# Attention in quarter tiles of the array, and mixing in plain float32

## The chip, the cores and the metric

The kernel runs on one core of a Trainium2 chip. TensorE multiplies matrices (weights are loaded first, then the moving operand streams through), ScalarE computes activations, VectorE elementwise operations, GpSimd (POOL) and SyncE (SP) mostly issue DMAs. The metric is device time in microseconds, the median of several runs.

## The reference, cut to what matters

```python
# attention: q, k, v are (4, 12, 448, 64)
scores = scale * np.matmul(q, k.transpose(0, 1, 3, 2))
scores = cap * np.tanh(scores / cap)
scores = scores - np.max(scores, axis=-1, keepdims=True)
attn = np.exp(scores)
attn = attn / (np.sum(attn, axis=-1, keepdims=True) + 1e-09)
x = np.matmul(attn, v)                  # then to (4, 448, 768)
# mixing over the tokens, rank 32, then two big products
xt = x.transpose(0, 2, 1)
h = xt @ U @ V                          # U (448, 32), V (32, 448)
u = x + h.transpose(0, 2, 1)
ch = np.maximum(u @ w_ch1, 0.0) @ w_ch2 # (768, 3072), (3072, 768)
out = u + ch
```

## The kernel before, in words

The program first lists tasks (`Plan.task`), each with engines, assumed durations, a priority and a mode (the tile shape on TensorE; a change of mode is charged `SWITCH`). `simulate` walks through time, always starting on a free engine the ready task of the lowest priority number for which buffers are free. The order that comes out is the order of instructions on each engine, so each engine's queue runs in that fixed order. `RANK` shifts priorities by kind of task, `SLOW` stretches some assumed DMA latencies.

There are 24 head pairs (4 batches, 6 pairs of 2 heads, 64 wide each). `four` handles four pairs at a time, `normalize` and `mixin` two pairs at a time; two pairs are called a half here, and there are twelve.

Scores (L488 to 495): keys lie on the output partitions. Of the 448 keys of a pair three tiles have 128 keys, and the two heads use the upper and the lower 64 rows of the array (two 64x128 matmuls side by side). The last 64 keys of two pairs share a narrow tile of four 64x64 matmuls (`t == 3`). So a half has seven tiles, two of which fill one buffer `th` of 128 x 1792. ScalarE applies tanh to each tile (L498) and exp to the buffer (L508).

P.V (L518 to 537): `rest` does the last 64 keys of two pairs in four 64x64 matmuls into two accumulators `o`, `o2`, then `full` does, for each pair, three tiles of 128 keys in two 128x64 matmuls each (two heads side by side in the array's columns). VectorE adds the exps up into `es` for the row sums (L540). Each accumulator is copied to `u` by ScalarE or VectorE (L555). From `SUMS` on the narrow tile is not added on VectorE, but summed on TensorE (L576).

Row sums (L571 to 577) are matmuls with ones, 128x32. Their reciprocals go through three small DMAs on POOL (`spread`, `put`, `get`) and scale `u` (`norm`, L602).

Mixing (`mixin`, L607 to 667): two transposes of `u` (112 tokens at a time, four matmuls each), a copy as fp32r `high`, the remainder `low` on VectorE (L635), `products` with U in four fp32r matmuls for each of the two steps (L640), the copy `ys` and its remainder (L651), `mix` with V, 128x128, in fp32r (L660), and the sum into `u` (L664).

The big products (L851, L916, L1049), seven products in place of eight, need PSUM banks of the score tiles and so begin when the attention is done with them; the last mixings run among them. Their operands are made on ScalarE and VectorE by `operands`, `strassen_weights` and `weights`, partly under the attention. The last block's outputs are added to `u` by VectorE, or copied by ScalarE and added by an accumulating DMA of POOL (`onto`, L1076).

## Time and profile before

| | us |
|---|---|
| median of 3 runs | 858.47 (857.27 to 858.69) |
| the profiled execution | 853.6 |
| its span, first to last instruction | 851.8 |
| TensorE busy | 840.4 (99%) |
| VectorE busy | 691.0 (81%) |
| ScalarE busy | 527.6 (62%) |
| POOL busy | 146.1 (17%) |

The shares are means over stages. A stretch of the windows view gives the busy time of each engine in one stage. On the timeline of TensorE the end of a matmul is modelled, so the step from a start to the next start says more than a duration; a count in a chunk is instructions, and a float32 matmul is two of them. In a row, `128*64` is rows by columns of the array that a matmul uses.

### The profile page before, as it was taken

To read this page: it belongs to the slowest core of one execution; us is meant where nothing else is said; L and a number is where in the kernel's file an instruction comes from. 1 tells how busy PE (TensorE), PEld (TensorE's weight loads), DVE (VectorE), ACT (ScalarE), POOL (GpSimd) and SP (SyncE) were. 2 spreads that over 40 slices of the span, in tenths; PEclk is the share of its full clock that TensorE was granted. 3 is DMA by queue.
4 is the path that set the end of the run, shared out by engine and by line. 5 is a ranking of instruction groups with operands and counts; after the bars stand their busy time and mean duration, and the time that the engine had idled before them with its cause. 6 is when DMAs were issued, how large, how long until landed. Compare 5 with 4: busy or idle time off the path is not lost. (4 is left out here: it accounts for less than half of the span.)

```text
span 851.8 us, 11737 instructions
## 1 busy us (share of the span) xinstructions
PE 840.4 (99%) x4264; PEld 671.4 (79%) x4264; DVE 691.0 (81%) x1144; ACT 527.6 (62%) x789; POOL 146.1 (17%) x188
## 2 busy tenths in 40 slices
PE   9999999998999999999999999999999999999998
PEld 5334334346899999999999899999999999999997
DVE  2799889999887777877778699789888788888786
ACT  7999899885555355545555465456655555656472
POOL 0111111111022122122122122102111111111142
PEclk9999999999999999999999999999999999999999
DMA  6752443423578878787877866714427354262479
GB/s 225 241 172 84 160 148 96 146 68 93 183 190 259 245 188 249 191 265 211 231 231 207 252 162 151 215 48 120 114 36 179 68 143 93 53 170 42 122 136 224
DMA packets 51354, 136.51 MB, mean 160 GB/s; under 512 B 6720, under 2 KB 27104, under 8 KB 51296
## 3 DMA queue, kind: packets, MB, share of 16 engines
q1 hardware_dynamic: 23024, 79.29, 28.3%
q0 software_dynamic: 21360, 37.59, 24.6%
q10 hardware_dynamic: 6912, 18.88, 5.7%
q8 instruction: 33, 0.54, 0.3%
q14 instruction: 25, 0.20, 0.1%
HBM read 79.28 MB, written 24.47 MB: 122 GB/s over the span
## 5 line engine op out<-in xcount | busy, mean ns | idle before, releaser
L851 PE MATMUL mm<-x,ws 128*128 128x448 f32 x1512 | 332.7, 367 | 1.4 <-ACT cx L284 0.8
L851 PEld LDWEIGHTS mm<-x,ws 128*128 128x128 f32 x1512 | 283.3, 188 | 27.3 <-ACT cx L284 1.2
L916 PE MATMUL mm<-g,w 128*128 128x448 f32 x864 | 187.0, 366 | 0.6 <-DVE cx L864 0.3
L916 PEld LDWEIGHTS mm<-g,w 128*128 128x128 f32 x864 | 162.0, 188 | 15.0 <-ACT st L284 0.9
L1049 PE MATMUL mm<-g,w 128*128 128x448 f32 x696 | 154.9, 366 | 0.0
L284 ACT ACTIVATE st<-mm 128x448 f32<-128x448 f32 x133 | 72.4, 544 | 113.7 <-PE mm L916 55.2
L1049 PEld LDWEIGHTS mm<-g,w 128*128 128x128 f32 x696 | 130.6, 188 | 11.8
L929 POOL DMA_DIRECT2D u<-st x72 | 62.5, 868 | 268.9 <-ACT st L284 263.8
L1084 POOL DMA_DIRECT2D u<-st x57 | 49.4, 866 | 224.1 <-ACT st L284 161.4
L498 ACT ACTIVATE th<-sc,qsc 128x896 f32<-128x896 f32 x84 | 80.3, 1005 | 11.9 <-PE sc L493 11.7
L493 PE MATMUL sc<-qk 64*128 64x448 f32 (+1 forms) x384 | 77.8, 573 | 0.0
L508 ACT ACTIVATE th<-th,capt 128x1792 f32<-128x1792 f32 x42 | 75.2, 1790 | 0.8
L921 DVE TENSOR_TENSOR u<-u,mm 128x448 f32<-128x448 f32 x72 | 44.5, 618 | 21.6 <-PE mm L916 19.9
L534 PE MATMUL o<-th,vn 128*64 128x448 f32 x288 | 59.4, 548 | 0.0
L493 PEld LDWEIGHTS sc<-qk 64*128 64x128 f32 (+1 forms) x384 | 27.2, 175 | 37.2 <-issue 18.9
L343 DVE SCALAR_TENSOR_TENSOR wa<-wa,wr 128x768 int32<-128x768 int32 (+2 forms) x50 | 46.7, 935 | 11.1 <-ACT wa L335 10.3
L698 DVE TENSOR_TENSOR ws<-ta,ws 128x384 fp32r<-128x384 f32 x96 | 53.0, 552 | 3.2 <-ACT ws L284 2.9
L1079 DVE TENSOR_TENSOR u<-u,mm 128x448 f32<-128x448 f32 x57 | 35.0, 619 | 23.3 <-PE mm L1049 21.7
L540 DVE TENSOR_TENSOR es<-es,th 128x896 f32<-128x896 f32 (+1 forms) x44 | 47.5, 1082 | 6.0 <-ACT th L508 5.5
L335 ACT ACTIVATE wa<-wr 128x768 f32<-128x768 f32 (+2 forms) x50 | 44.1, 884 | 3.8 <-DVE wr L340 2.4
L534 PEld LDWEIGHTS o<-th,vn 128*64 128x64 f32 x288 | 18.5, 136 | 32.8 <-issue 30.0
L284 ACT ACTIVATE ws<-ta 128x384 fp32r<-128x384 f32 x64 | 32.9, 519 | 15.2 <-PE mm L851 8.9
(118 smaller groups left out, 957.5 us busy)
## 6 DMA issues: line engine op xcount, KB each, us to landing
wr<-in_w SPq DMA_DIRECT2D x48, 768.0 KB, 5.7
u<-st POOLq DMA_DIRECT2D x129, 224.0 KB, 4.1
kept<-wa ACTq DMA_DIRECT2D x48, 384.0 KB, 5.8
qk<-in_qk SPq DMA_DIRECT2D x24, 448.0 KB, 4.0
wr<-kept SPq DMA_DIRECT2D x24, 384.0 KB, 3.7
wa<-kept SPq DMA_DIRECT2D x24, 384.0 KB, 4.0
vn<-in_v SPq DMA_DIRECT2D x12, 448.0 KB, 3.7
rb<-rd POOLq DMA_DIRECT2D x24, 224.0 KB, 3.7
```

The lines of the kernel that those rows point to most:

```text
L284: e.activation(out=out, in_=in_, func=func)
L493: nc.tensor.matmul(ps.t[out, a, :S], qks[c].t[hd, 1, 128 * t:min(S, 128 * t + 128)], qks[c].t[hd, 0], start=True, stop=True)
L498: nc.scalar.activation(out=th.t[:, j], in_=ps.t[:, :, :S], func=AF.Tanh, scale=self.qsc)
L508: nc.scalar.activation(out=th.t, in_=th.t, func=AF.Exp, scale=self.capt)
L534: nc.tensor.matmul(o.t[64 * a:64 * a + 64, :S], vn.t[:, 3 * i + t, a], th.t[:, j, a], start=False, stop=t == 2)
L540: e.tensor_tensor(out=out(), in0=in0(), in1=in1(), op=ALU.add)
L698: e.tensor_tensor(out=lo, in0=src(), in1=hi.bitcast(F32), op=ALU.subtract)
L851: nc.tensor.matmul(ps.t[:, :S], ws[p].t[:, wi, sl], xs[p].t[:, xi, d], start=fresh and n == 0, stop=n == 8, skip_group_check=not fresh)
L916: nc.tensor.matmul(ps.t[:, :S], w1[f].t[:, wi, sl], g[b, f].t[:, gi], start=f == fs[0] and i == 0, stop=f == fs[-1] and i == 2)
L929: nc.gpsimd.dma_start(out=u.t[:, d], in_=st.t, accum_op=ALU.add)
L1049: nc.tensor.matmul(ps.t[:, :S], w[:, wi, k, sl], g[gi][:, k], start=fresh and n == 0, stop=n == 5, skip_group_check=not fresh)
L1084: self.task({"POOL": 1000}, lambda: nc.gpsimd.dma_start(out=out(), in_=st.t, accum_op=ALU.add), r=[(st, 0)], w=[key], lat=6000, prio=-200)
```

## The change

Score tiles have 64 keys of each of the two pairs of a half: all seven are four 64x64 matmuls, a quarter of the array each. P.V runs tile by tile in the same shape, as seven tasks that all write both accumulators; V is laid out accordingly by the host. The exps of both pairs are summed in one `es`, all seven tiles on VectorE (`SUMS` is now past the last pair). The row sums are two 128x64 matmuls. The mixing is in plain float32: no remainders, all four token blocks in one `xx`, then eight products of 112x64, and a mix of four 64x64 matmuls for both pairs of a half; `ys` no longer shares the buffer of `sr`. The planner's priorities are set by stage and by half, U and V are kept as plain float32, the order of the first operands changes, and three more outputs of the last block are added by VectorE.

```diff
...
-EARLY = 5, 6, 2, 3, 4, 1, 7
+EARLY = 5, 6, 2, 3, 1, 7, 4
 
 ALONE = 12
-SUMS = 20
+SUMS = 24
...
-        self.an = Pool("an", {"sr": 1, "rb": 1}, side="right", shared={"ys": "sr"})
+        self.an = Pool("an", {"sr": 1, "rb": 1, "ys": 1}, side="right")
...
-        ust = self.ust = self.buf("ust", [TM, KT, 4, R], F32R, self.aq)
-        vst = self.vst = self.buf("vst", [128, S], F32R, self.aq)
+        ust = self.ust = self.buf("ust", [TM, KT, 4, R], F32, self.aq)
+        vst = self.vst = self.buf("vst", [128, S], F32, self.aq)
...
-            for i in range(3):
-                nc.vector.tensor_copy(ust.t[:, :, i], ur)
-            nc.vector.tensor_tensor(out=ust.t[:, :, 3], in0=ur, in1=ust.t[:, :, 0].bitcast(F32), op=ALU.subtract)
+            nc.vector.memset(ust.t[:, :, 1], 0.0)
+            nc.vector.tensor_copy(ust.t[:, :, 0], ur)
 
         def v_parts():
-            vr = a2.t[:, :S]
-            nc.vector.tensor_copy(vst.t, vr)
-            nc.vector.tensor_tensor(
-                out=vst.t[64:96], in0=vr[64:96], in1=vst.t[64:96].bitcast(F32), op=ALU.subtract)
+            nc.vector.tensor_copy(vst.t, a2.t[:, :S])
...
-        steps = [(0, 0), (0, 1), (0, 2), (1, 3), (1, 0), (1, 1), (1, 2), (2, 0), (2, 1), (3, 3), (2, 2), (3, 0), (3, 1), (3, 2)]
         where = {}
         for g in range(7):
             th = self.buf("th", [128, 2, 2, S], F32, *pools)
             pss = [self.psum("sc", 2), self.psum("sc2", 2)]
-            prio = prios[steps[2 * g][0]]
+            prio = prios[4 * g // 14 * 2]
             for j in range(2):
-                i, t = steps[2 * g + j]
-                where[i, t] = th, j
+                h, t = divmod(2 * g + j, 7)
+                where[h, t] = th, j
                 ps = pss[j]
-                cs = (i - 1, i) if t == 3 else (i,)
-
-                def scores(i=i, t=t, ps=ps, cs=cs):
-                    for c in cs:
-                        out = slice(64 * (c % 2), 64 * (c % 2) + 64) if t == 3 else slice(0, 128)
+
+                def scores(h=h, t=t, ps=ps):
+                    for i in range(2):
+                        qk = qks[2 * h + i]
                         for a in range(2):
                             hd = slice(64 * a, 64 * a + 64)
                             nc.tensor.matmul(
-                                ps.t[out, a, :S], qks[c].t[hd, 1, 128 * t:min(S, 128 * t + 128)], qks[c].t[hd, 0],
-                                start=True, stop=True)
+                                ps.t[64 * i:64 * i + 64, a, :S], qk.t[hd, 1, 64 * t:64 * t + 64], qk.t[hd, 0], start=True, stop=True)
...
-                r = [(qks[c], 0) for c in cs]
+                r = [(qks[2 * h + i], 0) for i in range(2)]
                 if j == 0:
-                    self.task({"PE": 750}, scores, r=r, w=[(ps, 0), (pss[1], "next")], prio=prio, mode="q" if t == 3 else "sc")
+                    self.task({"PE": 750}, scores, r=r, w=[(ps, 0), (pss[1], "next")], prio=prio, mode="q")
                 else:
-                    self.task({"PE": 750}, scores, r=[*r, (pss[1], "next")], w=[(ps, 0)], prio=-300, mode="q" if t == 3 else "sc")
+                    self.task({"PE": 750}, scores, r=[*r, (pss[1], "next")], w=[(ps, 0)], prio=-300, mode="q")
...
         for h in range(2):
-            vn, prio, i0 = vns[h], prios[2 * h], 2 * h
-            rth, rj = self.rest[p + i0 + 1] = where[i0 + 1, 3]
+            vn, prio, q = vns[h], prios[2 * h], p + 2 * h
+            whole = q + 1 < SUMS
+            ths = [where[h, t] for t in range(7)]
             os = [self.psum("o"), self.psum("o2")]
-
-            def rest(vn=vn, os=os, rth=rth, rj=rj):
-                for i in range(2):
-                    rows = slice(64 * i, 64 * i + 64)
-                    for a in range(2):
-                        nc.tensor.matmul(
-                            os[i].t[64 * a:64 * a + 64, :S], vn.t[rows, 6, a], rth.t[rows, rj, a], start=True, stop=False)
-
-            self.task({"PE": 760}, rest, r=[(vn, 0), (rth, rj)], w=[(o, 0) for o in os], prio=prio, mode="q")
-            for i, o in enumerate(os):
-                es = self.es[p + i0 + i] = self.buf("es", [128, 2, S], F32, *pools)
-                ts = [where[i0 + i, t] for t in range(3)]
-
-                def full(i=i, o=o, vn=vn, ts=ts):
-                    for t in range(3):
-                        th, j = ts[t]
+            es = self.es[q + 1] = self.buf("es", [128, 2, S], F32, *pools)
+            if not whole:
+                self.rest[q + 1] = ths[6]
+            at = lambda k: (lambda th=k[0], j=k[1]: th.t[:, j])
+            total = lambda es=es: es.t
+            for t in range(7):
+
+                def full(t=t, os=os, vn=vn, ths=ths):
+                    th, j = ths[t]
+                    for i in range(2):
+                        rows = slice(64 * i, 64 * i + 64)
                         for a in range(2):
                             nc.tensor.matmul(
-                                o.t[64 * a:64 * a + 64, :S], vn.t[:, 3 * i + t, a], th.t[:, j, a], start=False, stop=t == 2)
-
-                self.task({"PE": 2250}, full, r=[(vn, 0), *ts], w=[(o, 0)], prio=prio, mode="av")
+                                os[i].t[64 * a:64 * a + 64, :S], vn.t[rows, t, a], th.t[rows, j, a], start=t == 0, stop=t == 6)
+
+                self.task({"PE": 750}, full, r=[(vn, 0), ths[t]], w=[(o, 0) for o in os], prio=prio, mode="q")
 
                 def add(e, in0, in1, out):
                     e.tensor_tensor(out=out(), in0=in0(), in1=in1(), op=ALU.add)
 
-                at = lambda k: (lambda th=k[0], j=k[1]: th.t[:, j])
-                whole = lambda es=es: es.t
-                self.task({"DVE": 1090}, partial(add, in0=at(ts[0]), in1=at(ts[1]), out=whole), r=ts[:2], w=[(es, 0)],
-                    prio=prio, lock=True)
-                self.task({"DVE": 1090}, partial(add, in0=whole, in1=at(ts[2]), out=whole), r=ts[2:], w=[(es, 0)],
-                    prio=prio, lock=True)
-                if p < SUMS:
-                    rows = slice(64 * i, 64 * i + 64)
-                    some = lambda es=es, rows=rows: es.t[rows]
-                    self.task({"DVE": 1090}, partial(add, in0=some, in1=lambda rows=rows, rth=rth, rj=rj: rth.t[rows, rj], out=some),
-                        r=[(rth, rj)], w=[(es, 0)], prio=prio, lock=True)
-                b, q = divmod(p + i0 + i, NP)
-                u = self.u_bufs[b]
-                self.task({"DVE": 620, "ACT": 560}, lambda e, q=q, o=o, u=u: self.copy(e, u.t[:, q], o.t[:, :S]), r=[(o, 0)],
-                    w=[(u, q)], prio=prio)
+                if t and (whole or t < 6):
+                    self.task({"DVE": 1090}, partial(add, in0=at(ths[0]) if t == 1 else total, in1=at(ths[t]), out=total),
+                        r=ths[:2] if t == 1 else [ths[t]], w=[(es, 0)], prio=prio, lock=True)
+            b, q = divmod(q, NP)
+            u = self.u_bufs[b]
+            for i, o in enumerate(os):
+                self.task({"DVE": 620, "ACT": 560}, lambda e, q=q + i, o=o, u=u: self.copy(e, u.t[:, q], o.t[:, :S]), r=[(o, 0)],
+                    w=[(u, q + i)], prio=prio)
...
-        e = self.es[p - 1], self.es[p]
-        rth, rj = self.rest[p]
+        e = self.es[p]
         rest = p >= SUMS
+        rth, rj = self.rest.get(p, (e, 0))
...
         def sums():
-            for i in range(4):
-                nc.tensor.matmul(
-                    s.t[32 * i:32 * i + 32, :S], self.ones[:, 0], e[i % 2].t[:, i // 2], start=True, stop=not rest)
-            for i in range(4 if rest else 0):
-                nc.tensor.matmul(
-                    s.t[32 * i:32 * i + 32, :S], self.ones[:, 1 + i % 2], rth.t[:, rj, i // 2], start=False, stop=True)
+            half = self.ones[:, 1:].rearrange("p i r -> p (i r)")
+            for a in range(2):
+                nc.tensor.matmul(s.t[64 * a:64 * a + 64, :S], half, e.t[:, a], start=True, stop=not rest)
+            for a in range(2 if rest else 0):
+                nc.tensor.matmul(s.t[64 * a:64 * a + 64, :S], half, rth.t[:, rj, a], start=False, stop=True)
...
         u = self.u_bufs[b]
-        yp = None
         ks = [(u, 2 * pp), (u, 2 * pp + 1)]
+        xx = self.buf("xx", [TM, KT, 256], F32, self.aq)
         for t0 in (0, 2):
             tp = self.psum("misc")
-            yp = yp or self.psum("misc")
-            xx = self.buf("xx", [TM, 2, 2, 256], F32R, self.aq)
...
-            def view(tp):
-                return tp.t[:TM].rearrange("p (t n) -> p t n", t=2)
-
-            def high(e, tp=tp, xx=xx):
-                self.copy(e, xx.t[:, 0], view(tp))
-
-            def low(tp=tp, xx=xx):
-                nc.vector.tensor_tensor(out=xx.t[:, 1], in0=view(tp), in1=xx.t[:, 0].bitcast(F32), op=ALU.subtract)
-
-            def products(t0=t0, xx=xx):
+            def high(e, t0=t0, tp=tp):
+                self.copy(e, xx.t[:, t0:t0 + 2], tp.t[:TM].rearrange("p (t n) -> p t n", t=2))
+
+            self.task({"PE": 450}, transposes, r=[*ks, ("ident", 0)], w=[(tp, 0)], prio=prio, mode="mm")
+            self.task({"ACT": 600, "DVE": 690}, high, r=[(tp, 0)], w=[(xx, t0)], prio=prio)
+        yp = self.psum("misc")
+
+        def products():
+            for j in range(KT):
+                w = self.ust.t[:, j, :2].rearrange("p i r -> p (i r)")
                 for i in range(2):
-                    for j in range(2):
-                        nc.tensor.matmul(
-                            yp.t[:, :256], self.ust.t[:, t0 + j], xx.t[:, i, j], start=t0 + j + i == 0,
-                            stop=t0 + j == KT - 1 and i == 1)
-
-            self.task({"PE": 450}, transposes, r=[*ks, ("ident", 0)], w=[(tp, 0)], prio=prio, mode="mm")
-            self.task({"ACT": 600, "DVE": 690}, high, r=[(tp, 0)], w=[(xx, 0)], prio=prio)
-            self.task({"DVE": 690}, low, r=[(tp, 0), (xx, 0)], w=[(xx, 1)], prio=prio)
-            self.task({"PE": 480}, products, r=[(xx, 0), (xx, 1), (self.ust, 0)], w=[(yp, 0)], prio=prio, mode="mm")
-        ys = self.buf("ys", [128, 256], F32R, self.an)
-
-        def y_low():
-            nc.vector.tensor_tensor(
-                out=ys.t[32:64], in0=yp.t[32:64, :256], in1=ys.t[32:64].bitcast(F32), op=ALU.subtract)
-
-        self.task({"ACT": 380, "DVE": 400}, lambda e: self.copy(e, ys.t, yp.t[:, :256]), r=[(yp, 0)], w=[(ys, 0)], prio=prio)
-        self.task({"DVE": 420}, y_low, r=[(yp, 0)], w=[(ys, 0)], prio=prio)
+                    nc.tensor.matmul(
+                        yp.t[64 * i:64 * i + 64, :128], w, xx.t[:, j, 128 * i:128 * i + 128], start=j == 0, stop=j == KT - 1)
+
+        ys = self.buf("ys", [128, 128], F32, self.an)
+        self.task({"PE": 860}, products, r=[(xx, 0), (xx, 2), (self.ust, 0)], w=[(yp, 0)], prio=prio, mode="av")
+        self.task({"ACT": 270, "DVE": 220}, lambda e: self.copy(e, ys.t, yp.t[:, :128]), r=[(yp, 0)], w=[(ys, 0)], prio=prio)
+        hh = [self.psum("misc") for _ in range(2)]
+
+        def mix():
+            for i in range(2):
+                rows = slice(64 * i, 64 * i + 64)
+                for c in range(2):
+                    cs = slice(64 * c, 64 * c + 64)
+                    nc.tensor.matmul(hh[i].t[cs, :S], ys.t[rows, cs], self.vst.t[rows], start=True, stop=True)
+
+        self.task({"PE": 750}, mix, r=[(ys, 0), (self.vst, 0)], w=[(hh[0], 0), (hh[1], 0)], prio=prio, mode="q")
         for i in range(2):
-            hh = self.psum("misc")
-
-            def mix(i=i, hh=hh):
-                nc.tensor.matmul(hh.t[:, :S], ys.t[:, 128 * i:128 * i + 128], self.vst.t, start=True, stop=True)
-
-            def add(i=i, hh=hh):
+
+            def add(i=i):
                 x = u.t[:, 2 * pp + i]
-                nc.vector.tensor_tensor(out=x, in0=x, in1=hh.t[:, :S], op=ALU.add)
-
-            self.task({"PE": 210}, mix, r=[(ys, 0), (self.vst, 0)], w=[(hh, 0)], prio=prio, mode="mm")
-            self.task({"DVE": 620}, add, r=[(hh, 0)], w=[ks[i]], prio=prio)
+                nc.vector.tensor_tensor(out=x, in0=x, in1=hh[i].t[:, :S], op=ALU.add)
+
+            self.task({"DVE": 620}, add, r=[(hh[i], 0)], w=[ks[i]], prio=prio)
...
-                self.onto(ps, out, key, n % 2 if not final else n < 15)
+                self.onto(ps, out, key, n % 2 if not final else n < 12)
...
-            if -150 < t.prio < 0:
-                t.prio += next((r for x, r in RANK if stage.startswith(x)), 0)
+            if -150 < t.prio < -70:
+                p = t.prio + 100
+                x, early, late = next((r for r in RANK if stage.startswith(r[0])), ("", 0, 0))
+                t.prio += (early if p < ALONE else late) + SHIFT.get(x, {}).get(p, 0)
...
```

## Rows read from the trace of the kernel before

**Rows 1.** Windows: stretch, length, PE, PEld, DVE, ACT, POOL busy us (instructions), clock, DMA share, GB/s

```profile
43.00:197.00 154.00, 152.38 (x874) 61.65 (x875) 140.63 (x206) 139.82 (x140) 22.83 (x39) 1.00 0.41 124
60.00:180.00 120.00, 119.03 (x680) 48.11 (x680) 109.96 (x159) 111.78 (x114) 17.73 (x31) 1.00 0.38 115
197.00:225.00 28.00, 25.25 (x141) 21.17 (x140) 26.57 (x50) 16.90 (x33) 2.34 (x4) 1.00 0.28 88
225.00:500.00 275.00, 274.44 (x1349) 252.64 (x1348) 214.13 (x373) 140.19 (x242) 52.15 (x60) 1.00 0.81 230
```

**Rows 2.** Timeline of TensorE, one half of the steady stage: start us, us, line, shape, count

```profile
74.44 0.96 PE L573 MATMUL misc<-es,ones 128*32 128x448 f32 x8
75.33 0.65 PE L624 MATMUL misc<-ident,u 128*112 128x128 f32 x4
75.91 0.98 PE L522 MATMUL o<-th,vn 64*64 64x448 f32 x8
76.82 1.77 PE L493 MATMUL sc<-qk 64*128 64x448 f32 x8
78.52 0.74 PE L640 MATMUL misc<-xx,ust 112*128 112x256 f32 x4
79.10 0.60 PE L624 MATMUL misc<-ident,u 128*112 128x128 f32 x4
79.63 2.48 PE L534 MATMUL o<-th,vn 128*64 128x448 f32 x12
82.04 0.74 PE L640 MATMUL misc<-xx,ust 112*128 112x256 f32 x4
82.71 1.94 PE L493 MATMUL sc<-qk 64*128 64x448 f32 x12
84.58 2.48 PE L534 MATMUL o<-th,vn 128*64 128x448 f32 x12
86.98 0.68 PE L660 MATMUL misc<-vst,ys 128*128 128x448 f32 x2
87.59 1.77 PE L493 MATMUL sc<-qk 64*128 64x448 f32 x8
89.30 0.96 PE L573 MATMUL misc<-es,ones 128*32 128x448 f32 x8
```

**Rows 3.** Timeline of TensorE: sums of another half and of the eighth after it

```profile
58.49 0.96 PE L573 MATMUL misc<-es,ones 128*32 128x448 f32 x8
...
182.84 0.96 PE L573 MATMUL misc<-es,ones 128*32 128x448 f32 x8
183.61 0.94 PE L576 MATMUL misc<-th,ones 128*32 128x448 f32 x8
184.48 1.77 PE L493 MATMUL sc<-qk 64*128 64x448 f32 x8
```

**Rows 4.** Timeline of TensorE's weight loads in one 128x64 chunk, third wave on

```profile
45.53 0.14 PEld L534 LDWEIGHTS o<-th,vn 128*64 128x64 f32 x2 [0.23 <-issue]
45.91 0.14 PEld L534 LDWEIGHTS o<-th,vn 128*64 128x64 f32 x2 [0.23 <-issue]
```

**Rows 5.** Groups by line and form: busy us, mean ns of one, idle before

```profile
L498 ACT ACTIVATE th<-sc,qsc 128x896 f32<-128x896 f32 x84 | 80.3, 1005 | 11.9 <-PE sc L493 11.7
L508 ACT ACTIVATE th<-th,capt 128x1792 f32<-128x1792 f32 x42 | 75.2, 1790 | 0.8
L540 DVE TENSOR_TENSOR es<-es,th 128x896 f32<-128x896 f32 x24 | 26.1, 1086 | 5.6 <-ACT th L508 5.5
L635 DVE TENSOR_TENSOR xx<-misc,xx 112x512 fp32r<-112x512 f32 x24 | 16.4, 681 | 1.1 <-ACT xx L284 0.8
L651 DVE TENSOR_TENSOR ys<-misc,ys 32x256 fp32r<-32x256 f32 x12 | 5.0, 418 | 0.4
L286 DVE COPY u<-o 128x448 f32<-128x448 f32 x15 | 9.3, 622 | 3.7 <-PE o L534 3.6
```

**Rows 6.** Timeline of TensorE behind the attention: start us, us, idle before

```profile
204.55 0.51 PE L640 MATMUL misc<-xx,ust 112*128 112x256 f32 x2 [0.70 <-ACT xx L284]
```

120 lines of the change are left out of this document (77 added, 43 removed).

## Prediction

> **What bounds the kernel now.** I read the windows by stage first, to see which engine has no time left in each. From 43 to 197 us, the steady stage of the attention, TensorE is busy 152.38 of 154.00 us, VectorE 140.63 and ScalarE 139.82 [rows 1]. From 225 us on the products of the last block hold it, 274.44 of the next 275 us [rows 1]; the change touches none of these products, so what it can move lies ahead of 225 us. The granted clock is 1.00 (the level of 2.4 GHz) in every stretch of the table, so no term here is a term of the clock.
>
> A busy TensorE need not work at its peak, so the second view is its timeline in the steady stage, of which I use only the step from one start to the next start. One half of a group of four head pairs (four heads, two pairs) repeats between two row sums. Its steps [rows 2]: sums 0.89, transposes 0.58 and 0.53, rest of P.V 0.91, the two full P.V chunks 2.41 and 2.40, mixing products 0.58 and 0.67, a chunk of two score tiles 1.70, a chunk of one full and one narrow score tile 1.87, mix 0.61. Seven score buffers fill in two halves, two of them mixed, so a mean half has 2.5 x 1.70 + 1.87 = 6.12 of scores. The sum is 0.89 + 1.11 + 0.91 + 4.81 + 1.25 + 6.12 + 0.61 = 15.70 us. Eight halves in a row took (182.84 - 58.49) / 8 = 15.54 us each [rows 3]. So the period is the sum of TensorE's steps to 1%: nobody else sets it.
>
> What is in a step? A P.V chunk of three tiles takes 2.41, the rest chunk of one tile 0.91 [rows 2]: a tile costs (2.41 - 0.91) / 2 = 0.75, and a chunk 0.16 more, once. That 0.16 is what a change of tile shape costs: the mixed score chunk, with a change inside, is 0.17 longer than the plain one, 1.87 against 1.70 [rows 2]. A mean half has 3.5 score chunks, one change inside, and nine other chunks, so 13.5 changes or about 2.2 us, a seventh of the period.
>
> **The change, part by part.** *Tiles.* Scores and P.V keep their number of tiles, seven and seven a half, each now four 64x64 matmuls where a full one was two. The rest chunk is such a tile, 0.91 alone, and so 0.75 and one 0.16 if it splits as the full ones do. The trace never shows two quarter tiles back to back; bounds 0.75 and 0.91 each. I take 0.75, from the row nearest to it: within a 128x64 chunk the loads of the next wave issue 0.38 us apart, 45.53 and 45.91, the stream time of a wave, and hide [rows 4]. The Trainium skill speaks against this: "TensorE: Matmul & The Clock Gate", Part 3 (row and column tiling), says that a weight load overlaps running matmuls only when its row group differs, and quarter tiles share row groups in twos. The 128x64 chunk above shares them too, and its rows do not agree; by the rule the result would be rival B.
>
> *Changes of shape.* Scores, P.V and the mix now have one shape, so a half leaves it only for sums, transposes and products: three excursions, in and out, 6 x 0.16 = 0.96; with the two transposes apart 8 x 0.16 = 1.28.
>
> *Sums.* Two 128x64 matmuls for four 128x32, the price of one tile: 0.75 (the old chunk 0.89 less 0.16 is 0.73) [rows 2].
>
> *Mixing.* Transposes as before, 1.11 less two changes, 0.79. The products become eight float32 matmuls of 128 columns, two at a time: by the stream, 4 x 0.75 x 128/448 = 0.86. If their sixteen loads do not hide, the nearest row is the transposes chunk, four loads in 0.53 - 0.16 = 0.37, so 1.48. I take 1.0, nearer to the stream, since loads hid in the 128x64 chunk. The mix is one more quarter tile, 0.75 for 0.61.
>
> *A half after:* 15 x 0.75 + 0.75 + 0.79 + 1.0 = 13.79, and 0.96 to 1.28 of changes: 14.75 to 15.07, against 15.70. I take 14.85, so -0.85. The window of 154 us holds ten mixings and ten halves of P.V: -8.5 us (bounds, with those of the products and the changes: 15.55 and 14.61 a half, -1.5 to -11).
>
> *The other engines under it.* VectorE loses both subtractions of the mixing, 2 x 0.681 and 0.418 a half [rows 5], 1.8 us, or 18 us of its 140.63. ScalarE has (80.3 + 75.2) / 12 = 12.96 us of tanh and exp a half that nothing removes [rows 5]. From 60 to 180 us it was busy 111.78 of 120.00 [rows 1], 14.48 in 15.54, so 1.5 us a half were copies and the like; at 14.85 all of it still fits, at 97%, and copies can go to VectorE, which has just been given 1.8. The cover is gone near a period of 13.5 to 14.5, not at 14.85.
>
> *Last row sums.* The last two halves summed their rest on TensorE, 0.87 each (183.61 to 184.48) [rows 3]; that goes, -1.7 us, and four VectorE adds of 1.086 more take its place [rows 5]. They lie beside the last P.V, under the 18 us that VectorE was given; uncovered they cost up to 4.3.
>
> *Start.* The first score tile needs two head pairs instead of one. The program issues the second load right behind the first. No row shows the gap between their landings; between 0 and a score chunk, 1.70 [rows 2], I take +0.5, nearer to 0, since the program loads the scale of the first tanh between the two.
>
> *Behind the attention.* Two mixings run among the big products, whose shape the old mixing shared (128 wide). The new ones leave it: products 1.0 + 0.32 against 1.25 less two changes, 0.93, mix 0.75 + 0.32 against 0.61 less one, 0.45: +0.39 and +0.62, so +1.0 each, +2.0. Against that stand waits for the two-step copies, 0.70 at 204.55 and one more like it [rows 6], in a stretch with 25.25 of 28.00 us busy [rows 1]: -1.0, bounds 0 and -2.7.
>
> *The rest.* The order in which operands of the big products are made, their priorities, and three sums of the last block that move from ScalarE and POOL's accumulating DMA to VectorE: TensorE is full beside them (274.44 of 275), so 0 within 1 either way. No DMA is added; POOL's and SP's queues keep their entries. Rank, shift and latency tables only reorder.
>
> *New waits.* Both P.V accumulators now end on the same tile, and the next half's first P.V tile waits for both copies, 0.622 each [rows 5]; the mix needs two misc banks at once, and the products wait for both transposed copies. Behind such a wait all of TensorE's queue stands, and ScalarE's tanh behind that. Old steps show three chunks between a half's last P.V and the next rest chunk (86.98, 87.59, 89.30) [rows 2], which cover it. Bounds 0 and 1 us a half, taken as +1.0 in all.
>
> *Sum:* -8.5 - 1.7 + 0.5 + 2.0 - 1.0 + 1.0 = -7.7, about -8 us. The profiled execution took 853.6 us (span 851.8 and 1.8 around it), so 846 by its measure. The median of the runs is 858.47, 4.9 above it; the same -8 there gives 850.5.
>
> **The rivals.** *A: ScalarE takes over as the bound.* If its share of copies stays, 14.48 a half, and it gets no further than 96% busy, a half takes 15.1: gain (15.54 - 15.1) x 10 = 4.5, 854. For it: the lowest idle after TensorE's in the stretch from 60 to 180 us [rows 1]. Against: every copy has a VectorE form, and score tiles of 0.75 reach it sooner than behind chunks of 2.41.
>
> *B, slower: quarter tiles do not stream.* Each pays its own 0.16, as the lone rest chunk did: 15 x 0.91 + 0.75 + 0.79 + 1.0 and 3 x 0.16 for the excursions is 16.67, +0.97 on 15.70, ten halves, +9.7; with the other terms (+0.8) 869. It decides from the point where a tile costs 0.82 and not 0.75: 15 x 0.07 eats the 1.0 that the shapes give. For it: eight loads and eight matmuls in 0.75 us, twice as dense as before. The Trainium skill's rule on loads, named above, points the same way. Against: the loads at 45.53 and 45.91 [rows 4].
>
> *C: the new waits eat it.* One copy and its two latencies uncovered a half, 0.8 to 1 us: 858.5, no change. For it: in-order queues, and the same two banks for every mixing step. Against: only 1.6 of 154 us idle before, with as many hand-overs.
>
> **How the numbers follow.** Forecast 0.62, 850.5 (845 to 855 by the bounds that are likely together); A 0.14; B 0.08; C 0.13; anything else slower 0.03. A measurement of this kernel can tell about 0.2%, 1.7 us, from no change. Faster: forecast and A, 0.76. Same: most of C, 0.12. Slower: B, the rest, a little of C, 0.12. The range takes in the forecast's bounds, A, and C's middle, 843.5 to 859.0, and leaves out B and the far end of C.
>
> **What would show it.** Right: two adjacent quarter tiles on TensorE step 0.75 apart and 1.5 for two; from one half's row sums to the next 14.7 to 15.1; six to eight changes of shape a half; the first big product at about 188 us, and not at 197, where the steady window ends [rows 1]; products step near 1.2 with the change; VectorE less busy over the attention. Wrong: quarter tiles at 0.9; TensorE idle ahead of P.V or the mix with a copy as releaser; ScalarE at 97% or more; the attention shorter, but the big products later idle for weights or operands.

## The result, and the profile after

| | before | after |
|---|---|---|
| median of five runs, us | 857.47 (854.75 to 858.69) | 864.92 (862.11 to 869.60) |
| profiled execution, us | 853.6 | 862.11 |
| its span, us | 851.8 | 860.3 |
| first big product of the last block, us | 196.69 | 205.75 |

The ratio is 1.0099, with a 95% interval of 1.0075 to 1.0123: the kernel became slower by 1%, where 850.5 was forecast and the range ended at 859.0.

The first view is the page of the changed kernel, engine by engine: busy us, share of the span, instructions.

```profile
PE 838.8 (97%) x4944; PEld 671.0 (78%) x4944; DVE 679.1 (79%) x1122; ACT 522.5 (61%) x776; POOL 143.7 (17%) x185
```

TensorE was busy 838.8 us, and 840.4 before, while the span grew by 8.5. VectorE, at 679.1, has time to spare. So time was lost that is not work. The windows of the changed kernel say where (stretch, length, busy us of PE, PEld, DVE, ACT, POOL with instructions, granted clock, DMA share, GB/s); the first and third answer to [rows 1].

```profile
43.00:197.00 154.00, 142.72 (x1356) 58.27 (x1352) 126.24 (x181) 131.40 (x129) 21.16 (x37) 0.99 0.41 125
139.00:147.00 8.00, 7.18 (x60) 3.90 (x64) 7.75 (x13) 4.33 (x5) 1.35 (x3) 0.79 0.04 5
197.00:225.00 28.00, 27.29 (x196) 19.35 (x189) 24.43 (x44) 21.62 (x37) 3.92 (x7) 1.00 0.33 105
240.00:260.00 20.00, 16.82 (x74) 14.89 (x74) 14.56 (x27) 10.21 (x19) 4.32 (x5) 0.91 0.73 189
```

In the steady stage TensorE is idle for 11.28 of 154 us; before it was 1.62 [rows 1]. No other engine took its place as the bound: VectorE and ScalarE are less busy than before too. What grew is waiting. The attention as a whole is 9.06 us longer (205.75 against 196.69 at the first big product), and from there to the end the two kernels take the same time, 654.6 and 655.1 us of their spans. The loss is all in the attention. The rows of TensorE that set its end, first of the kernel before, then of the changed one:

```profile
104.16 0.96 PE L573 MATMUL misc<-es,ones 128*32 128x448 f32 x8
...
196.69 2.09 PE L851 MATMUL mm<-x,ws 128*128 128x448 f32 x9
198.71 0.96 PE L573 MATMUL misc<-es,ones 128*32 128x448 f32 x8
...
204.84 0.97 PE L588 MATMUL misc<-es,ones 128*64 128x448 f32 x4 [0.45 <-DVE es L561]
205.75 2.09 PE L858 MATMUL mm<-x,ws 128*128 128x448 f32 x9
```

Now the timeline of TensorE in a half of the changed kernel that goes well, the answer to [rows 2] (start us, us, line, shape, count):

```profile
71.34 0.97 PE L588 MATMUL misc<-es,ones 128*64 128x448 f32 x4
72.24 0.98 PE L555 MATMUL o<-th,vn 64*64 64x448 f32 x8
...
77.53 1.75 PE L519 MATMUL sc<-qk 64*64 64x448 f32 x16
79.21 1.09 PE L650 MATMUL misc<-xx,ust 112*64 112x128 f32 x16
80.24 0.98 PE L555 MATMUL o<-th,vn 64*64 64x448 f32 x8
81.04 0.93 PE L663 MATMUL misc<-vst,ys 64*64 64x448 f32 x8
81.79 1.68 PE L519 MATMUL sc<-qk 64*64 64x448 f32 x16
83.29 2.44 PE L555 MATMUL o<-th,vn 64*64 64x448 f32 x24
85.66 0.60 PE L588 MATMUL misc<-es,ones 128*64 128x448 f32 x2
```

By the step from one start to the next: the sums 0.90, three P.V tiles 2.37, two score tiles 1.50 (81.79 to 83.29), the mix 0.75, the products 1.03. A tile of four small matmuls costs 0.75 wherever the next step has its shape. The half takes 14.32 us; eight halves of before took 15.54 each [rows 3]. The row sums of all twelve halves stand at 25.65, 39.39, 55.92, 71.34, 85.66, 99.07, 119.96, 134.06, 158.16, 172.25, 191.73 and 204.84. Before, the sixth stood at 104.16 and the twelfth at 198.71. So the changed kernel was 5.1 us ahead after six halves, and lost 11.2 over the next six (105.8 against 94.6). The remaining 2.9 are nine big products that before ran ahead of its last sums, and none does now. Three of the late halves are long: 20.9, 24.1 and 19.5 us.

What stands in them? The same view from the last score tile ahead of the first long gap to the sums at its end (a bracket is idle time before the step, and what ended it), with SyncE's queue below it:

```profile
107.89 0.93 PE L519 MATMUL sc<-qk 64*64 64x448 f32 x8
108.65 0.92 PE L555 MATMUL o<-th,vn 64*64 64x448 f32 x4
110.41 4.35 PE L555 MATMUL o<-th,vn 64*64 64x448 f32 x42 [0.85 <-ACT u L316]
114.24 0.58 PE L519 MATMUL sc<-qk 64*64 64x448 f32 x2
114.60 0.54 PE L555 MATMUL o<-th,vn 64*64 64x448 f32 x2
114.61 2.03 PE L519 MATMUL sc<-qk 64*64 64x448 f32 x14
117.02 0.98 PE L519 MATMUL sc<-qk 64*64 64x448 f32 x8 [0.37 <-ACT th L523]
118.84 0.98 PE L555 MATMUL o<-th,vn 64*64 64x448 f32 x8 [0.84 <-ACT th L533]
119.96 0.97 PE L588 MATMUL misc<-es,ones 128*64 128x448 f32 x4
...
108.85 1.21 SPq L495 DMA_DIRECT2D qk<-in_qk  x2
```

The score tile at 107.89 is the last that reads the two q/k buffers of its half; at 108.85 SyncE issues the loads into them, the first of which is for the second pair of the next half. The next score tile, which needs that pair, runs at 114.24. Until then TensorE has only P.V tiles left, six in a row (48 instructions, one of them behind a wait of 0.85 for the copy of an accumulator). Then score tile, tanh and exp run one behind the other, with TensorE waiting for the tanh at 117.02 and for the exp at 118.84: the last P.V tile of the half lies in the same exp as the first of the next. From 107.89 to 119.96 the steps hold 88 instructions, 44 small matmuls of one shape or eleven tiles, with one change at the end 8.4 us; they took 12.1: 3.7 lost. The same place in the next long half shows the wait for the load itself:

```profile
151.14 0.93 PE L519 MATMUL sc<-qk 64*64 64x448 f32 x4
152.45 1.72 PE L519 MATMUL sc<-qk 64*64 64x448 f32 x12 [0.38 <-DMA qk<-in_qk]
155.21 0.98 PE L519 MATMUL sc<-qk 64*64 64x448 f32 x8 [1.04 <-ACT th L523]
157.03 0.98 PE L555 MATMUL o<-th,vn 64*64 64x448 f32 x8 [0.84 <-ACT th L533]
158.16 0.97 PE L588 MATMUL misc<-es,ones 128*64 128x448 f32 x4
```

Four tiles and a change of shape, 3.2 us by the steps, in 7.0 (151.14 to 158.16): 3.8 lost. The third long half has the same four tiles in 6.7 us, from 185.05 to 191.73, with 0.73 of wait for the load: 3.5 lost. The three together lose 11.0 us.

The second place stands in the same trace: TensorE, VectorE and POOL around 139 us.

```profile
134.96 1.73 PE L519 MATMUL sc<-qk 64*64 64x448 f32 x16
139.82 1.96 PE L635 MATMUL misc<-ident,u 128*112 128x128 f32 x8 [3.13 <-DVE u L615]
141.71 1.67 PE L555 MATMUL o<-th,vn 64*64 64x448 f32 x8
143.20 1.67 PE L519 MATMUL sc<-qk 64*64 64x448 f32 x16
144.81 1.09 PE L650 MATMUL misc<-xx,ust 112*64 112x128 f32 x16
...
138.67 1.09 DVE L615 TENSOR_TENSOR u<-u,rb 128x896 f32<-128x896 f32 x1 [3.73 <-DMA rb<-rd]
...
130.72 1.05 POOL L610 DMA_DIRECT2D rb<-rd  x2 [3.98 <-DMA rd<-r]
```

The transposes of the mixing need the attention scaled by the row sums, and the sums go to DRAM and come back spread over the partitions, by POOL's DMA. The DMA, whose issue took from 130.72 to 131.77, let the scaling start at 138.67, about 7 us later where 3.7 is the median. TensorE's queue has the transposes next, and stands for 3.13 us. What follows is slow as well: transposes 1.89 instead of 1.01, a P.V tile 1.49 instead of 0.80, at a granted clock of 0.79 over the 8 us of the window, and of 0.51, the level of 1.2 GHz, from 139.8 to 143.2. The transposes at 88.23, with no wait, took that 1.01, and the tile behind them that 0.80. From 134.96 to 144.81, 9.85 us passed for two score tiles (1.66), the transposes (1.01), a P.V tile (0.80) and two score tiles (1.61), 5.1 us: 4.8 lost.

11.0 and 4.8 are 15.8 us. The prediction had the first big product at about 188, and it stands at 205.75, 17.8 later: these two places are most of it.

TensorE's waits, summed over the run (line and what ended the wait; us in total, times, longest), give the same two places:

```profile
PE misc L635 <- DVE u L615: 3.3, 2, 3.1
PE mm L923 <- ACT st L316: 3.2, 1, 3.2
PE sc L519 <- DMA qk<-in_qk: 2.8, 3, 1.7
PE o L555 <- ACT th L533: 2.5, 3, 0.8
```

The second row is a third place, behind the attention; it returns in the experiments.

### The profile page after: what moved, and what is told of

It is laid out like the page before. It is cut to its first block, busy times and chain, and to the rows that moved or that the text cites. A ratio compares the mean times of both kernels' runs of the same rounds, so it can differ in the third digit from the quotient of the medians.

```text
span 860.3 us, 13045 instructions
## 1 busy us (share of the span) xinstructions
PE 838.8 (97%) x4944; PEld 671.0 (78%) x4944; DVE 679.1 (79%) x1122; ACT 522.5 (61%) x776; POOL 143.7 (17%) x185
## 4 chain that ended last, share of the span: by engine, by line
PE 83%; DMA 9%; DVE 4%; issue 2%; ACT 1%; POOL 1%; SPq 0%; ACTq 0%; POOLq 0%; DVEq 0%
PE mm L858 36%; PE mm L923 20%; PE mm L1056 18%; DMA rb<-rd 3%; PE o L555 3%; PE sc L519 3%; DMA rd<-r 2%; DMA qk<-in_qk 1%; DMA u<-st 1%; DVE es L561 1%; DMA r<-sr 1%; PE misc L635 1%; PE misc L650 1%; PE misc L663 1%; DVE u L615 1%
## 5 line engine op out<-in xcount | busy, mean ns | idle before, releaser
L936 POOL DMA_DIRECT2D u<-st x72 | 62.7, 871 | 263.8 <-ACT st L316 256.1
L1091 POOL DMA_DIRECT2D u<-st x54 | 46.8, 867 | 221.1 <-ACT st L316 158.7
L519 PE MATMUL sc<-qk 64*64 64x448 f32 x672 | 76.8, 546 | 4.6 <-DMA qk<-in_qk 2.8
L561 DVE TENSOR_TENSOR es<-es,th 128x896 f32<-128x896 f32 x60 | 65.0, 1084 | 17.3 <-ACT th L533 16.6
L555 PE MATMUL o<-th,vn 64*64 64x448 f32 x672 | 74.2, 549 | 3.5 <-ACT th L533 2.5
L375 DVE SCALAR_TENSOR_TENSOR wa<-wa,wr 128x768 int32<-128x768 int32 (+2 forms) x50 | 46.7, 936 | 20.5 <-ACT wa L367 20.4
L519 PEld LDWEIGHTS sc<-qk 64*64 64x64 f32 x672 | 24.8, 133 | 44.7 <-issue 29.2
L928 DVE TENSOR_TENSOR u<-u,mm 128x448 f32<-128x448 f32 x72 | 44.6, 619 | 16.4 <-PE mm L923 14.2
L1086 DVE TENSOR_TENSOR u<-u,mm 128x448 f32<-128x448 f32 x60 | 36.9, 620 | 23.4 <-PE mm L1056 21.7
L555 PEld LDWEIGHTS o<-th,vn 64*64 64x64 f32 x672 | 24.1, 133 | 37.2 <-issue 26.6
L316 ACT ACTIVATE ws<-wa 128x384 fp32r<-128x384 f32 x61 | 30.8, 519 | 27.2 <-PE mm L858 26.7
```

The lines of the kernel that those rows point to most:

```text
L316: e.activation(out=out, in_=in_, func=func)
L519: nc.tensor.matmul(ps.t[64 * i:64 * i + 64, a, :S], qk.t[hd, 1, 64 * t:64 * t + 64], qk.t[hd, 0], start=True, stop=True)
L555: nc.tensor.matmul(os[i].t[64 * a:64 * a + 64, :S], vn.t[rows, t, a], th.t[rows, j, a], start=t == 0, stop=t == 6)
L561: e.tensor_tensor(out=out(), in0=in0(), in1=in1(), op=ALU.add)
L936: nc.gpsimd.dma_start(out=u.t[:, d], in_=st.t, accum_op=ALU.add)
L1091: self.task({"POOL": 1000}, lambda: nc.gpsimd.dma_start(out=out(), in_=st.t, accum_op=ALU.add), r=[(st, 0)], w=[key], lat=6000, prio=-200)
```

## The experiments

The theory from the trace had two parts. *Buffers* (Q in the expectations): a score tile now reads both pairs of a half, so both q/k buffers are held to the half's last score tile; with the three buffers that are left from the third group on, the second load of a next half can be issued only then, and the pipeline drains. *Scale wait*: the broadcast of the row sums comes later than the planner reckons, and the transposes stand at the head of TensorE's queue. The rivals were that the new mixing itself, or the shorter chunks, made the loss. Each kernel was timed beside the kernel before on one chip; ratios are to it, with 95% intervals. Not all were timed on the same chip, so a difference of two times can be off by a microsecond or two.

**A fourth q/k buffer, order kept.** Only the loads move forward in SyncE's order, to where the fourth buffer is free.

```diff
+        self.ap.bufs = dict(self.ap.bufs, qk=4)
...
+                users = [i for i, t in enumerate(order) if bufs[n - 4] in t.bufs]
...
+                    order.insert(to, order.pop(at))
```

> The changed kernel with a fourth q/k buffer in the attention's pool; the order on TensorE, VectorE, ScalarE and POOL is kept, only the q/k loads stand earlier in SyncE's queue (each right behind the last score tile that used the buffer four loads back). Theory Q (both pairs of a half now hold their q/k buffers until its last score tile, so with three buffers the second load of the next half starts late and the tile that the next half shares with this one drains the pipeline): the three long halves of 20.9, 24.1 and 19.5 us shrink to 14 to 16, the attention ends 10 to 15 us sooner, 850 to 855. Rival N (the chain of small DMAs behind the row sums sets the pace, as the wait of 3.1 us for the scaled u shows): under 4 us gained, 861 to 865. Rival S (ScalarE's tanh and exp set it): no gain, 863 to 866.

868.04 us, 1.0113 (1.0054 to 1.0172): no gain. TensorE now waits for a q/k load only once, at the start, but the same drains stand at the same places:

```profile
111.12 4.35 PE L555 MATMUL o<-th,vn 64*64 64x448 f32 x42 [0.85 <-ACT u L316]
119.54 0.98 PE L555 MATMUL o<-th,vn 64*64 64x448 f32 x8 [0.84 <-ACT th L533]
```

The order was laid out for three buffers: the score tile stands behind six P.V tiles in TensorE's queue, buffer or no buffer. Its own load is long done. It belongs to the eighth half, whose second pair is the sixteenth load; SyncE issues that at 92.74, and the two loads of 109.56 are for the ninth half:

```profile
92.74 0.33 SPq L495 DMA_DIRECT2D qk<-in_qk  x1
...
109.56 1.19 SPq L495 DMA_DIRECT2D qk<-in_qk  x2
```

The expectation (850 to 855 by the theory) failed. For the buffers this run decides nothing; it shows that the drain is written into the order of an in-order queue.

**The same, with the order planned anew.**

```diff
-        self.ap = Pool("ap", {"qk": 3, "vn": 2, "th": 4, "es": 2}, side="right")
+        self.ap = Pool("ap", {"qk": 4, "vn": 2, "th": 4, "es": 2}, side="right")
```

> The changed kernel with a fourth q/k buffer, and the planner makes its order anew with it. Theory Q: 848 to 855, the long halves gone. Rival N and rival S: 860 or more. If the order itself matters (its priorities were set for three buffers) it differs from the run with the kept order by several us in either direction.

858.84 us, 1.0018 (0.9995 to 1.0041), between the two ranges that were expected. The long halves are gone, as the theory had it: 15.5, 16.3, 14.8, 17.2, 15.5 and 15.2 for the last six. The first big product moves from 205.75 to 197.29. What is left on TensorE:

```profile
PE misc L635 <- DVE u L615: 4.5, 3, 3.0
PE mm L923 <- ACT st L316: 3.3, 1, 3.3
```

The scale wait is there, one of 3.00 us. And behind the attention some of the gain is given back: from the first big product to the end of the span 660.5 us, against 654.6.

**Mixing alone**, on the kernel before: the new constants and the new mixing, with the planner's step that can take two banks at once; tiles, sums and start stay.

```diff
...
-        for i in range(2):
-            hh = self.psum("misc")
...
+        hh = [self.psum("misc") for _ in range(2)]
...
+        self.task({"PE": 750}, mix, r=[(ys, 0), (self.vst, 0)], w=[(hh[0], 0), (hh[1], 0)], prio=prio, mode="q")
```

> The kernel before with the new mixing alone (plain float32, eight products of 112x64, mix of four 64x64), scores, P.V and row sums as before. Theory Q: the mixing is not what costs; per half products 1.03 for 1.25 and mix 0.91 for 0.61 on TensorE, 1.8 us less on VectorE, so within 3 us of the kernel before, 855 to 860. Rival M (the mixing needs two banks at once and one long chain, and this is what costs): 862 to 868.

863.94 us, 1.0059 (1.0036 to 1.0082): slower, in the range of rival M and not of the theory; the run without its scale wait, below, decides between them. TensorE's longest waits, in the order of this kernel's own lines (L603 scales, L541 adds for the sums):

```profile
PE misc L623 <- DVE u L603: 4.2, 3, 2.3
PE misc L574 <- DVE es L541: 3.2, 3, 1.8
```

The scale wait again, where the kernel before has it once with 1.7 us.

**Tiles alone**: the changed kernel with the mixing of before.

```diff
...
+            def low(tp=tp, xx=xx):
+                nc.vector.tensor_tensor(out=xx.t[:, 1], in0=view(tp), in1=xx.t[:, 0].bitcast(F32), op=ALU.subtract)
...
```

> The changed kernel with the old fp32r mixing: quarter tiles, P.V tile by tile and the new row sums stay, three q/k buffers. Theory Q: the long halves stay, 862 to 868. Rival M: 850 to 857, since what costs is gone.

865.87 us, 1.0087 (1.0060 to 1.0114), with long halves of 19.7, 18.5 and 22.7 us. The long halves come with the tiles and not with the mixing, as the theory of the buffers has it.

**The order for four buffers, with three.** The order of the replanned kernel; each q/k load is put behind the last reader of the buffer that it must wait for.

```diff
+        self.ap.bufs = dict(self.ap.bufs, qk=3)
...
+                last = max(i for i, t in enumerate(order) if bufs[n - 3] in t.bufs)
+                at = order.index(load)
+                if last > at:
+                    order.insert(last, order.pop(at))
```

> The order that was planned for four q/k buffers (the run e2), emitted with three: only the q/k loads stand later in SyncE's queue, each behind the last score tile that frees its buffer. Theory Q (the buffer itself is what the long halves come from, not the priorities): TensorE waits for q/k loads at three or more halves, the halves behind 100 us grow from 15.8 to 17 or more, and 864 to 872 comes out, against 858.8 of e2. Rival O (the order is what matters, and three buffers serve it as well): 857 to 861.

884.70 us, 1.0324 (1.0282 to 1.0367), 26 us above the same order with four buffers. Most of it is one row:

```profile
PE sc L519 <- DMA qk<-in_qk: 21.0, 8, 5.9
```

This is the disputed cost by itself: same instructions, same order of TensorE, one buffer fewer. It was larger than expected. The changed kernel has six P.V tiles saved up for the time of the load (108.65 and 110.41), and this order, made for four buffers, has not; that is argued, not tried.

**The changed kernel without the scale wait.** The scaling multiplies u by itself and so waits for no broadcast; the DMAs run as before. Only the instruction changes, not the tasks that the planner orders, so TensorE's instructions come in the same order as in the changed kernel.

```diff
-            nc.vector.tensor_tensor(out=x, in0=x, in1=rb.t, op=ALU.mult)
+            nc.vector.tensor_tensor(out=x, in0=x, in1=x, op=ALU.mult)
```

> The changed kernel in its own order; the scaling of u by the row sums' reciprocals multiplies u by itself and so waits for no DMA. All DMAs are still issued. Left out: the scaling itself. Rival N (the small DMAs behind the row sums set the pace): TensorE's wait of 3.1 us at 139.8 and the slow clock behind it go, and the halves shorten all along, 850 to 858. Theory Q: that one wait goes, the long halves at 108, 150 and 185 us stay, 858 to 862 against 864.9.

859.89 us, 1.0036 (1.0014 to 1.0058): 5 us below the changed kernel, and the three long halves stay, 20.6, 20.5 and 19.5.

**Four buffers and no scale wait**, both edits; the order is that of the run with four buffers.

```diff
-        self.ap = Pool("ap", {"qk": 3, "vn": 2, "th": 4, "es": 2}, side="right")
+        self.ap = Pool("ap", {"qk": 4, "vn": 2, "th": 4, "es": 2}, side="right")
...
-            nc.vector.tensor_tensor(out=x, in0=x, in1=rb.t, op=ALU.mult)
+            nc.vector.tensor_tensor(out=x, in0=x, in1=x, op=ALU.mult)
```

> The run e2 (four q/k buffers, planned anew) with the same scaling by u itself. Left out: the scaling. Its three waits for the scaled u, 4.5 us together, go. If both causes add up, 853 to 856 against 858.8 of e2, and the first big product stands near 192 us. If the attention's gain is given back behind it (the first big products wait for their copies and DMAs), the first big product stands near 192 us too, but the time stays at 857 to 860.

848.92 us, 0.9897 (0.9865 to 0.9929), below both ranges that were expected. In the attention this is the kernel that the prediction had worked out: nothing but TensorE's steps. TensorE's steady stage, 119.60 of 120.00 us busy, by the windows:

```profile
60.00:180.00 120.00, 119.60 (x1195) 50.07 (x1197) 108.63 (x156) 114.87 (x111) 18.78 (x32) 1.00 0.45 129
```

The third row sums start at 56.61 and the eleventh at 175.18: eight halves in 118.57 us, 14.82 each. Its first big product is at 189.28. Behind it stands the third place: TensorE waits 3.5 us once for ScalarE to copy an output of the second product into a staging buffer, as in the changed kernel.

**Four buffers, and the planner told the truth.** Nothing is left out: the planner, which reckoned 2.5 to 4.5 us for the landing of the broadcast, reckons 5, and so puts the transposes later.

```diff
-                t.lat = GOT.get(t.bufs[0].i, t.lat)
+                t.lat = 5000
```

> Four q/k buffers, and the planner reckons 5.0 us to landing for the broadcast of the reciprocals in place of 2.5 to 4.5, so the transposes stand later in TensorE's queue; nothing is left out. If both waits are the cause (theory Q and N together), TensorE's waits for q/k and for the scaled u stay under 2 us, the halves behind 57 us take 14.8 to 15.2, the first big product stands at 189 to 193 us and the time is 848 to 854. If the wait only moves (to the accumulators' copies or to ScalarE), 857 to 861.

847.87 us, 0.9916 (0.9885 to 0.9947), which beats the kernel before. Nine row sums from 57.13 to 175.65, 14.8 a half; first big product 189.75. TensorE in the steady stage, and what is left of its wait for the scaling:

```profile
43.00:197.00 154.00, 151.31 (x1490) 66.43 (x1483) 139.31 (x205) 143.08 (x147) 23.34 (x40) 1.00 0.42 127
...
PE misc L635 <- DVE u L615: 1.7, 1, 1.7
```

**The kernel before with a fourth q/k buffer**, a control.

```diff
-        self.ap = Pool("ap", {"qk": 3, "vn": 2, "th": 4, "es": 2}, side="right")
+        self.ap = Pool("ap", {"qk": 4, "vn": 2, "th": 4, "es": 2}, side="right")
```

> The kernel before with a fourth q/k buffer, as a control. Its halves work through one pair after the other and free a buffer in the middle of a half, so theory Q says that it has no use for the fourth: 855 to 860, the same. If it gains 3 us or more, the buffer is a general remedy and not what the change ran into.

856.11 us, 0.9991 (0.9970 to 1.0012): the same, and so is TensorE's order that the planner makes with it. The old kernel works through a half pair by pair, so the first pair's buffer is free before the half ends, and a fourth is worth nothing to it. The buffer is needed by the change alone.

**Mixing alone without the scale wait**, and **the kernel before without it**, each with the edit on the scaling.

```diff
-            nc.vector.tensor_tensor(out=x, in0=x, in1=rb.t, op=ALU.mult)
+            nc.vector.tensor_tensor(out=x, in0=x, in1=x, op=ALU.mult)
```

> The kernel before with the new mixing alone (863.9), and the scaling multiplies u by itself, so that it waits for no DMA. Left out: the scaling. If the 6 us that the mixing alone cost were waits for the scaled u (2.3 us at 44 us, and the slow clock behind it), 856 to 859; if they are work on TensorE or the chain of the mixing itself, 861 to 864.

851.06 us, 0.9931 (0.9910 to 0.9952), 12.9 below the mixing alone (11 by the two ratios), and below both ranges that were expected. So neither the work of the new mixing nor its chain (rival M) made it slower.

> The kernel before, and the scaling multiplies u by itself, so that it waits for no DMA: what the same wait costs there, as a control for e6, e7 and e10. Left out: the scaling. TensorE waited 1.9 us in all for the scaled u before (1.69 at 43.6 us and 0.24 later), so 854 to 857 if only those go; 849 to 852 would say that the wait cost the kernel before as much as the others, and that e10's gain is not the mixing's.

853.34 us, 0.9956 (0.9932 to 0.9980). That is between the two ranges that were expected. So the wait costs the kernel before about 4 us, the changed one 5, the one with four buffers 9.9, and the mixing alone 11 to 13. These are more than TensorE's own waits for the scaled u (1.7, 3.3, 4.5 and 4.2 us). VectorE stands for the broadcast too, with all that is behind the scaling in its queue: 4.3, 9.3, 14.2 and 15.3 us in these four kernels, which rise as the costs do. That this is the rest of the cost is argued from it, not tried. With the wait taken out on both sides, the new mixing is worth -2.3 us (851.06 against 853.34), which is not clear of the noise, as the intervals of the two ratios overlap, and the whole change with four buffers -4.4 (848.92 against 853.34), whose intervals just part.

**The first twelve outputs of the second product added by VectorE alone**, on top of the four buffers and the late scale: no staging buffer and no accumulating DMA where the third wait stood.

```diff
-                if k % 2:
+                if k % 2 and fs[0] > 0:
```

> The run e8, and the first twelve outputs of the second big product are all added by VectorE, where every second went through a copy by ScalarE and an accumulating DMA. The stall of 3 to 3.5 us that all runs of the changed kernel show behind 240 us (ScalarE's copy waits for the DMA that still holds its buffer) and the slow clock behind it should go: 3 to 5 us less than e8. If VectorE, which then has six adds of 0.62 more in its fullest stretch, becomes the bound there, no gain or 1 to 2 us more.

845.33 us, 0.9859 (0.9838 to 0.9881), the fastest: 2.5 below the run it was made from, where 3 to 5 were expected. The two lie close: the runs of the other range from 844.52 to 856.14, and the profiled executions are 0.3 apart (845.98 and 845.70). In that other trace the third place has another form. ScalarE stands 5.72 us, until 223.91, for an accumulating DMA, and TensorE then 2.23 us, until 224.51, for an operand that ScalarE copies, with no wait of 3 us behind 240. Here that wait is gone, and 0.2 us for the staging buffer are left; TensorE waits 1.07 us for VectorE instead, until 214.83. The first big product is at 189.28, for 189.75.

## Why the prediction was wrong, step by step

*The work of TensorE: right.* "A tile costs 0.75": 1.50 for two tiles, 2.37 for three with the change of shape behind them (2.41 by the prediction's sum). Products 1.03, sums 0.90, mix 0.75. The period of 14.85 was measured at 14.82 once both waits were out, and at 14.8 in the kernel that leaves nothing out; the first big product then stands at 189.3 to 189.8, for about 188. The gain was taken from 15.70, the prediction's own sum of steps, where the trace had 15.54, so that it is 0.72 a half and 7 us over ten halves, for 8.5.

*Rival B: wrong.* Quarter tiles stream. The two loads of a wave share row groups with those of other waves, and cost nothing that the steps show, as in the 128x64 chunk before [rows 4].

*Rival A, ScalarE as the bound: not seen.* In the kernel that runs at 14.82 a half ScalarE is busy 114.87 of 120 us, 96%, as the prediction's 97% had it, and TensorE is still the one with no time left.

*VectorE: right in sign.* The new mixing alone takes 14 us from it in the steady stage (126.43 busy of 154 without the scale wait, 140.63 before [rows 1]), for 18 reckoned.

*"New waits", +1.0 in all, bounds 0 and 1 us a half: the step that failed.* It listed what a P.V tile and a mix newly wait for: accumulator copies, banks, transposed copies. Of these the trace shows one, 0.85 at 110.41, inside the first drain. It did not ask how long a buffer that is read must live. "The program issues the second load right behind the first" was used for the start alone, and "No DMA is added; POOL's and SP's queues keep their entries" was true and beside the point: the entries stay, and the moment at which two of them can be issued moves to the end of a half. Three halves lose 3.7, 3.8 and 3.5 us there. The runs with three and four buffers in one order (884.70 and 858.84) and the control (856.11) show this cause; that the fourth buffer did nothing in the order made for three shows that it acts through the order of the queue.

*The scale wait: left out.* The prediction took 1.6 us of idle TensorE in the old steady stage as proof that the hand-overs had room. The room was the old order's own, and it too paid 1.7 us once. After, one such wait cost 3.13 us of standing and about 1.6 of slow steps behind it. The order had left about as much time there as before: 16.7 us from the row sums (119.96) to where the transposes could have started, against 16.84 in a half of the kernel before (58.49 [rows 3] to 75.33 [rows 2]). What was longer was the landing, about 7 us for 3.7. Runs with the wait taken out, and with the planner's figure mended, show the cause. But it is not new: it is worth about 4 us in the kernel before and 5 in the changed one, so of the 7.5 us between these two it explains about one, and the buffers the rest. At four buffers, where the pace is that of the prediction, it is worth 9.9, and the prediction had nothing for it.

*Start: too small.* +0.5 was forecast, from 0 to 1.7. The first tanh starts at 9.15 and started at 6.62 before, +2.5. The second half of the first tile waited for the second load:

```profile
8.14 1.72 PE L519 MATMUL sc<-qk 64*64 64x448 f32 x12 [1.68 <-DMA qk<-in_qk]
```

By the first row sums it is made up (25.65 against 27.19), so it moved the result little.

*Last row sums: right.* The two chunks at the end save 0.73 each (1.64 before from 198.71 to 200.35, 0.91 now from 204.84 to 205.75), 1.5 for 1.7.

*Behind the attention: right in sum, with a hole.* The stretch from 197 to 225 has 27.29 us of TensorE busy for 25.25 [rows 1], and the products of the mixings wait for no copy there (216.48 and 231.29 in the timeline), so the waits for the two-step copies [rows 6] went as forecast. Then 3.2 us are lost around 250, where the forecast had "0 within 1". Rows of TensorE and ScalarE there:

```profile
251.04 5.48 PE L923 MATMUL mm<-g,w 128*128 128x448 f32 x18 [3.18 <-ACT st L316]
...
250.44 0.54 ACT L316 ACTIVATE st<-mm 128x448 f32<-128x448 f32 x1 [4.88 <-DMA u<-st]
```

ScalarE stood for an accumulating DMA that still read the staging buffer. Two were under way, issued by POOL at 241.26 and 244.92; landings of this kind took 3.1 to 9.6 us, 4.0 by the median. Without staging for these outputs the best kernel is 2.5 us faster by the median than the same without that edit, with the reserve named there; how much of that is this wait is not shown.

*Rival C: the nearest.* It had the kind right, waits that eat the gain behind in-order queues, with a chance of 0.13. It had the place wrong, and its price of one copy a half (8 to 10 us over the attention) was too small: 15.8 were lost.

*What stays open.* The two costs don't add: taking out the scale wait is worth 5 us with three buffers and 9.9 with four, and the fourth buffer 6 with the wait and 11 without. The wait is taken out of one and the same order each time, so these two prices are its own; the fourth buffer comes with a new order, and the runs don't separate the buffer from what that order does elsewhere. The planner's new priorities are part of the change and stayed in every kernel with the new tiles; what they cost or give alone was not tried. Against the kernel before without its wait, the change with four buffers and without it gains 5.4 us at the first big product (189.28 for 194.68) and gives 3.2 back behind it, where TensorE waits 3.49 us for the staging buffer: the spans are 2.2 apart (848.1 for 850.3). Why the broadcast took about 7 us was not tried; q/k and weight loads were issued in the microseconds ahead of it.

## What to carry to other kernels

When a change makes one step read two inputs instead of one, write down for each input buffer from when to when it is held, and compare with the number of buffers, before summing the work that is saved. When a period gets shorter, list every chain beside it that does not get shorter with it (a DMA to DRAM and back) and ask if its result still comes before its reader is first in line. A buffer added to a kernel with a fixed order shows nothing until the order is made again: test the two together, and the buffer alone on the old kernel as a control.

## What the runs showed of the hardware

Four 64x64 float32 matmuls of 448 columns, one for each quarter of the array, step 0.75 to 0.76 us from tile to tile, and their loads (133 ns by the median of the 672 for the scores) hide. The Trainium skill, "TensorE: Matmul & The Clock Gate", Part 3, lets a load overlap running matmuls only where its row group differs, though it also names a load into the background weight buffer as one that goes ahead. Quarter tiles share row groups in twos, and these rows do not agree with the "only"; no run here shows which buffer a load went to.

A wait can cost TensorE more than its own length. Behind 3.13 us of standing the granted clock was 0.51 from 139.8 to 143.2, the lower of its two levels (1.2 and 2.4 GHz), and a P.V tile took 1.49 us instead of 0.80; behind 3.18 us at 251 it was 0.54 from 253 to 256. Not every wait of this length did that: behind the 3.00 us in the run with four buffers planned anew, which end at 152.45, it was 1.00 from 152 to 160. Behind the waits of 0.84 to 1.04 us in the drains it was 1.00 too (108 to 122, 151 to 160 and 185 to 195).

Landings vary by a factor of two: 3.3 to 7.3 us for the same 224 KB broadcast within one execution of the changed kernel, with 3.7 as the median, and 3.3 to 6.8 in the kernel before. One late landing is enough for an in-order queue to stand.
